# A gated attention and MLP decode step: the query weight loaded by eight transfers instead of one, the result written by four

## Chip, core and metric

The kernel runs on one core of a Trainium2 chip. A core has five engines that run their own instruction streams beside each other: TensorE (PE, matrix products; its weight loads are listed apart as PEld), VectorE (DVE), ScalarE (ACT), GpSimd (POOL) and SyncE (SP, which here only issues transfers). Sixteen DMA engines move data between the chip's main memory (HBM) and the on-chip buffer SBUF, which has 128 partitions. SP and ACT each have a queue from which they issue transfers. Engines wait for each other, and for transfers, by semaphores.

The metric is the device time of one execution in microseconds (us), the median of several. Lower is better.

## What is computed

One decode step for a batch of four tokens: attention over the last 4096 rows of a key and value cache, and a small gated MLP, mixed by a sigmoid gate. Cut to what matters:

```
B, D, Hq, Hkv, Dh, W, F = 4, 512, 32, 8, 128, 4096, 1792        # bfloat16
q      = (x @ wq)                       # wq: [512, 4096], 4 MB
scores = q . k_cache[:, :, -W:, :] * Dh ** -0.5
o      = softmax(scores) . v_cache[:, :, -W:, :]
a      = o @ wo                         # wo: [4096, 512], 4 MB
gate   = x @ W_gate;  up = x @ W_up
b      = (gate * (gate > 0) * up) @ W_down
g      = sigmoid((x * gate_w).sum(-1))
out    = g * a + (1 - g) * b            # [4, 1, 512]
```

The used parts of the two caches are 32 MB each, and the weights some 13 MB: about 81 MB are read in all, and 4 KB are written.

## The kernel before, in words

**Tiles and stages.** The eight sets `s` = 0 to 7 are half a batch entry each: four key/value heads of one token, 4 MB of keys and 4 MB of values. Keys lie in `Ksb` and values in `Vsb`, two buffers each, so that set `s + 2` can only be loaded when set `s` has been used. For each set, TensorE transposes the keys (`kt`, L340), ScalarE and VectorE copy the transposed tiles back into `Ksb` (L345, L347), TensorE makes the scores (L373), VectorE masks them (L381), ScalarE takes the exponentials (L410), VectorE transposes them (L417), and TensorE multiplies them with the values (L429) and combines the heads (L442). The MLP weights take the key and value buffers after the last sets.

**`Wbig`.** One tile of 128 partitions with 32 KB each holds `wq` at first. Row group `p` of `wq`, its rows 4p to 4p + 3, which are 32 KB in one piece, goes to partition `p`. When the query projection `qproj` (L457, 128 products) has read it, the same tile takes `wo`, in four transfers (`WO_CUTS`, L260).

**Order of the transfers.** All large ones are issued by SP, in the order of the program: `wq` (L245), K0, K1, V0, K2, V1 and so on (L236, L240), then the MLP weights (L250 to L255) and `wo`. ACT issues only two small ones at the start, the rows `x` (four rows of 1 KB, L243) and `gate_w` (one row, L244).

**How waits are written.** `P.op` and `P.dma` append to a list for each engine, with a name for the event and the names of events that it waits for. A DMA has a semaphore of its own (or one for its buffer), which counts 16 when it has landed. `plan` drops waits that an engine has already made. `P.op(engine, None, None, waits)` is a bare wait. Each engine's list becomes its instruction stream within one `nc.Block()`, at whose end the engines meet in a barrier that GpSimd gathers and releases.

**The start.** TensorE's first product (L306) waits for `x`, `gate_w` and an identity matrix that GpSimd makes; then come the gate (L315, L318, L319) and `qproj`, which waits for `("WQ",)`. The result of `qproj` goes through VectorE and TensorE (L461, L464, L468) and GpSimd (`place_q`, L357) to the scores of the first set, which also need K0.

**The end.** `gateup` and the last values are followed by the products with `W_down` (L545) and `wo` (L553), which add up in one bank of PSUM; VectorE copies it to `outs` (L557), a tile of 128 partitions of which every eighth holds a result row: row `8 b` of the 32 partitions of column block `c` has columns 128 c to 128 c + 127 of token `b`. SP writes these 16 pieces of 256 bytes with one transfer (L558) and waits for it (L559; the profile shows that wait under L562, the block's end). After that comes the barrier.

## Time and profile before

| what | value |
|---|---|
| median of 3 runs | 197.73 us (197.53 to 197.76) |
| the profiled execution, device time | 197.38 us |
| its span in the profile | 195.7 us |
| mean granted TensorE clock | 0.889 of full speed |
| busy: PE, DVE, ACT, POOL | 140.6, 103.6, 91.5, 7.9 us |
| read from HBM | 81.01 MB, 414 GB/s over the span |
| `wq` issued by SP, first product that reads it | 0.81 us, 13.08 us |
| last product, copy to `outs`, write issued by SP | 192.74, 193.19, 193.51 us |

The span runs from the first to the last instruction in the profile, and the device time has 197.38 - 195.7 = 1.7 us around it. Busy times of engines overlap, so they don't add up to the span. "PE busy" is the time in which matrix products were in the pipeline, whatever the clock.

### The profile page before, as it was taken

How to read it: one execution, taken by the hardware profiler on the slowest of the kernel's cores; microseconds unless marked ns; L12 is line 12 of the kernel's file. 1: busy time of each engine (PE TensorE's matmuls, PEld its weight loads, DVE VectorE, ACT ScalarE, POOL GpSimd, SP SyncE). 2: the span in 40 equal slices, each digit the busy share in tenths (PEclk: the TensorE clock that was granted, in tenths of full speed). 3: DMA queues.
4: the chain of work that ended last, by engine and by line, in shares of the span. 5: the costliest groups of instructions: out<-in, count | busy, mean ns of one | idle time of the engine just before them, and what ended most of it. 6: DMA issues, size and time to landing. Idle time of an engine off the chain costs nothing.

```text
span 195.7 us, 4263 instructions
## 1 busy us (share of the span) xinstructions
PE 140.6 (72%) x1858; PEld 107.7 (55%) x1858; DVE 103.6 (53%) x278; ACT 91.5 (47%) x108; POOL 7.9 (4%) x39
## 2 busy tenths in 40 slices
PE   0134199968889919992999399929992999498634
PEld 0034197535567518751976286528752875397533
DVE  2102025888599456945585659456945584741200
ACT  2000058698398409760886098509750976220000
POOL 7400000000000000000000000000000000000000
PEclk9999999999999996997599879996996699965855
DMA  6999999999999999999999999999999999999991
GB/s 215 449 429 452 429 449 442 425 429 437 432 422 429 425 429 429 427 429 425 435 429 435 429 429 430 429 429 429 429 429 429 435 411 425 450 431 415 422 385 59
DMA packets 3498, 81.19 MB, mean 415 GB/s; under 512 B 409, under 2 KB 414, under 8 KB 670
## 3 DMA queue, kind: packets, MB, share of 16 engines
q1 hardware_dynamic: 3476, 81.01, 96.8%
q8 instruction: 9, 0.15, 0.3%
q14 instruction: 3, 0.02, 0.0%
q10 hardware_dynamic: 10, 0.01, 0.0%
HBM read 81.01 MB, written 0.00 MB: 414 GB/s over the span
## 4 chain that ended last, share of the span: by engine, by line
DMA 57%; PE 25%; ACT 9%; DVE 4%; issue 1%; SPq 1%
DMA Ksb<-in_A_k_cache_dram 46%; PE bank L340 16%; DMA Wbig<-in_A_wo_dram 12%; ACT Ksb L345 7%; PE bank L373 5%; DVE Ksb L347 2%; PE bank L429 2%; ACT sc L410 2%; PE bank L553 1%; PE bank L442 1%; DVE pT L417 1%; ACT L410 1%; DVE sc L381 1%; SPq L260 0%; DVE oq L450 0%
## 5 line engine op out<-in xcount | busy, mean ns | idle before, releaser
L345 ACT ACTIVATE Ksb<-bank 128x1024 bf16<-128x1024 bf16 x72 | 70.9, 1022 | 68.2 <-PE bank L340 68.0
L340 PE MATMUL bank<-identf,Ksb 128*128 128x128 f32 x512 | 81.1, 313 | 29.4 <-DMA Ksb<-in_A_k_cache_dram 24.0
L340 PEld LDWEIGHTS bank<-identf,Ksb 128*128 128x128 f32 x512 | 66.6, 161 | 44.1 <-DMA Ksb<-in_A_k_cache_dram 25.7
L347 DVE COPY Ksb<-bank 128x1024 bf16<-128x1024 bf16 x56 | 38.0, 685 | 41.8 <-PE bank L340 40.8
L381 DVE CUSTOM_DVE_ANT_0 sc<-bank,mask 128x512 bf16<-128x512 f32 x32 | 21.7, 684 | 9.6 <-PE bank L373 9.5
L429 PE MATMUL bank<-Vsb,pT 128*32 128x256 bf16 x512 | 20.8, 291 | 0.9 <-DMA Vsb<-in_A_v_cache_dram 0.9
L373 PE MATMUL bank<-Ksb,QSP 128*32 128x512 bf16 x256 | 19.4, 383 | 2.1 <-DVE Ksb L347 1.6
L410 ACT ACTIVATE sc<-sc,negmax 128x1024 bf16<-128x1024 bf16 x16 | 18.3, 1146 | 4.8 <-DVE negmax L402 4.7
L417 DVE STREAM_TRANSPOSE pT<-sc 128x1024 bf16<-128x1024 bf16 x16 | 19.7, 1237 | 1.3 <-ACT sc L410 1.0
L429 PEld LDWEIGHTS bank<-Vsb,pT 128*32 128x32 bf16 x512 | 13.2, 101 | 7.1 <-issue 3.3
L442 PEld LDWEIGHTS bank<-osb,Wsel 128*64 128x64 f32 x128 | 8.1, 138 | 4.6 <-issue 2.6
L442 PE MATMUL bank<-osb,Wsel 128*64 128x32 f32 x128 | 8.9, 224 | 1.2 <-DVE osb L434 1.2
L373 PEld LDWEIGHTS bank<-Ksb,QSP 128*32 128x32 bf16 x256 | 4.1, 94 | 9.4 <-DVE Ksb L347 4.4
L477 PE MATMUL bank<-xT,Ksb 128*128 128x4 bf16 x112 | 6.9, 199 | 1.8 <-DVE oq L450 1.8
L477 PEld LDWEIGHTS bank<-xT,Ksb 128*128 128x128 bf16 x112 | 6.8, 160 | 1.9 <-issue 1.9
L553 PE MATMUL bank<-Wbig,oq 128*32 128x128 bf16 x128 | 4.2, 311 | 4.1 <-DMA Wbig<-in_A_wo_dram 4.0
L357 POOL COPY QSP<-QS 128x64 bf16<-128x64 bf16 x8 | 1.8, 236 | 118.2 <-PE bank L373 107.4
L457 PE MATMUL bank<-xT,Wbig 128*128 128x4 bf16 x128 | 3.6, 166 | 4.0 <-DMA Wbig<-in_A_wq_dram 4.0
L306 PE MATMUL bank<-ident,xsb 5*128 5x5 bf16 x4 | 0.3, 167 | 7.9 <-DMA xsb<-in_gate_w_dram 7.9
L553 PEld LDWEIGHTS bank<-Wbig,oq 128*32 128x32 bf16 x128 | 3.1, 140 | 5.0 <-DMA Wbig<-in_A_wo_dram 5.0
L457 PEld LDWEIGHTS bank<-xT,Wbig 128*128 128x128 bf16 x128 | 3.5, 104 | 4.0 <-DMA Wbig<-in_A_wq_dram 4.0
L434 DVE COPY osb<-bank 128x256 f32<-128x256 f32 x8 | 3.4, 420 | 3.6 <-PE bank L429 3.6
(55 smaller groups left out, 47.0 us busy)
## 6 DMA issues: line engine op xcount, KB each, us to landing
Ksb<-in_A_k_cache_dram SPq DMA_DIRECT2D x8, 4096.0 KB, 22.9
Vsb<-in_A_v_cache_dram SPq DMA_DIRECT2D x8, 4096.0 KB, 32.0
Wbig<-in_A_wq_dram SPq DMA_DIRECT2D x1, 4096.0 KB, 12.2
Wbig<-in_A_wo_dram SPq DMA_DIRECT2D x1, 2048.0 KB, 20.2
Ksb<-in_B_W_gate_dram SPq DMA_DIRECT2D x1, 1792.0 KB, 17.9
Ksb<-in_B_W_up_dram SPq DMA_DIRECT2D x1, 1792.0 KB, 21.8
Vsb<-in_B_W_down_dram SPq DMA_DIRECT2D x1, 1792.0 KB, 15.6
Wbig<-in_A_wo_dram SPq DMA_DIRECT2D x1, 1280.0 KB, 22.8
```

The source lines that it names most:

```text
L340: P.op("pe", lambda e, bk=bk, cc=cc, c=c, s=s: e.transpose(bk[:, cc * 128:(cc + 1) * 128], kw[:, c * 128:(c + 1) * 128], identf[:, :]), (" ...
L345: P.op("act", lambda e: e.activation(dst, bk[:, :].bitcast(BF16), ACTF.Copy), ("KTC", s, i), [("KT", s, i)])
L347: P.op("dve", lambda e: e.tensor_copy(dst, bk[:, :].bitcast(BF16)), ("KTC", s, i), [("KT", s, i)])
L373: P.op("pe", lambda e, a=a, h=h: e.matmul(bk[32 * a:32 * a + 32, 0:512], QSP[:, s % 2, h, :], k4[:, 16 * bank:16 * bank + 16, 32 * a:32 * ...
L381: P.op("dve", lambda e: e.tensor_tensor_reduce(sc[:, s % 2, bank * 512:(bank + 1) * 512], bk[:, :], mask[:, :], 1.0, LOWEST, ALU.add, ALU.max,
L410: P.op("act", lambda e: e.activation(sc[:, par, k * PW:(k + 1) * PW], sc[:, par, k * PW:(k + 1) * PW], ACTF.Exp, bias=negmax[:, par:par + ...
L417: P.op("dve", lambda e: e.transpose(pT[:, par, k * PW:(k + 1) * PW], sc[:, par, k * PW:(k + 1) * PW]), ("PTT", s, k), [("EXP", s, k), ("PV ...
L429: P.op("pe", lambda e, c=c, g=g, col=col: e.matmul(OB[32 * g:32 * g + 32, 0:256], pT[:, par, col:col + 32], v3[:, 16 * k + c, :], start=(k ...
L442: P.op("pe", lambda e, k=k, lo=lo: e.matmul(FB[r, 256:288], Wsel[:, lo:lo + 64], osb[:, par, 32 * k:32 * k + 32], start=(k == 0), stop=(k ...
L457: P.op("pe", lambda e, h=h, t=t: e.matmul(FB[:, 64 + 4 * h:68 + 4 * h], Wq3[:, t, 128 * h:128 * h + 128], xT[:, t * 8:t * 8 + 4], start=(t ...
L477: P.op("pe", lambda e, W=W, i=i, t=t, col=col: e.matmul(FB[:, col:col + 4], W[:, t, i:i + NFT * 127 + 1:NFT], xT[:, t * 8:t * 8 + 4], star ...
L553: P.op("pe", lambda e, i=i, cb=cb: e.matmul(AB[32 * cb:32 * cb + 32, 0:128], oq[:, i, :], Wo3[:, i, cb * 128:(cb + 1) * 128], start=False, ...
```

## The change

Three things are changed; the rest is the same.

```diff
-        P.dma("sp", lambda e: e.dma_start(Wbig[:, :], A_wq.rearrange("(p t) w -> p (t w)", p=128)), ("WQ",))
+        for r in range(8):
+            P.dma("sp", lambda e, r=r: e.dma_start(
+                Wbig[r:128:8, :], A_wq.rearrange("(e r t) w -> r e (t w)", r=8, t=4)[r]), ("WQ", r))
...
-                        ("Q",) if (h == HQ - 1 and t == 3) else None, [("WQ",), ("XTC",), ("G",)])
+                        ("Q",) if (h == HQ - 1 and t == 3) else None, [("WQ", r) for r in range(8)] + [("XTC",), ("G",)])
...
-        P.dma("sp", lambda e: e.dma_start(out.rearrange("b o (c d) -> c (b o) d", d=128), outs[0:128:8, :]), ("OUT",), [("OUTS",)])
-        P.op("sp", None, None, [("OUT",)])
+        for c in range(4):
+            P.dma(("sp", "act")[c % 2], lambda e, c=c: e.dma_start(
+                out[:, 0, 128 * c:128 * c + 128], outs[32 * c:32 * c + 32:8, :]), ("OUT", c), [("OUTS",)])
+        P.op("pool", None, None, [("OUT", c) for c in range(4)])
```

- `wq` is loaded by eight transfers of SP, one after the other. Transfer `r` moves 16 rows of 32 KB to the partitions r, r + 8, ..., r + 120. The eight have a semaphore each, and the first product of `qproj` waits for all of them. Each partition gets the same bytes as before.
- The result is written by four transfers of four rows of 256 bytes, one for each column block: SP issues blocks 0 and 2, ACT blocks 1 and 3. Both wait for the copy to `outs`.
- GpSimd, and no longer SP, waits for the result's transfers, with four semaphores, at the end of its list.

## The prediction

> **What bounds the kernel now.** I read the page's slices first, then its list of queues, its chain, the list of transfers, the windows at the start, and the timeline at both ends. The slices:

> ```profile
> PE   0134199968889919992999399929992999498634
> DMA  6999999999999999999999999999999999999991
> GB/s 215 449 429 452 429 449 442 425 429 437 432 422 429 425 429 429 427 429 425 435 429 435 429 429 430 429 429 429 429 429 429 435 411 425 450 431 415 422 385 59
> ...
> q1 hardware_dynamic: 3476, 81.01, 96.8%
> ```

> The DMA row is full from the second slice to the last but one, at about 430 GB/s whatever is moved, while every engine has gaps. SP's queue (q1) fills 96.8% of sixteen engines' time. So the kernel is one long stream of 81 MB, and it ends a fixed tail after the stream.

> ```profile
> DMA 57%; PE 25%; ACT 9%; DVE 4%; issue 1%; SPq 1%
> ...
> Ksb<-in_A_k_cache_dram SPq DMA_DIRECT2D x8, 4096.0 KB, 22.9
> Vsb<-in_A_v_cache_dram SPq DMA_DIRECT2D x8, 4096.0 KB, 32.0
> Wbig<-in_A_wq_dram SPq DMA_DIRECT2D x1, 4096.0 KB, 12.2
> ```

> The chain gives DMA only 57% because it follows compute wherever a buffer had to come free. The transfer list shows that this compute is not the limit: a key set takes 22.9 us to land and a value set 32.0, where 4 MB at 430 GB/s take 4.194 / 0.430 = 9.75 us. Each is issued while one or two others are still ahead of it, so the stream does not run dry. The shortest reserve is at SP's first wait, which ends at 36.99 us in the timeline: 16.8 MB had been issued by then and about (36.99 - 1.8) x 0.43 = 15.1 MB moved, so 1.7 MB or 3.8 us were left. A microsecond that the stream loses at its head is therefore a microsecond at the end: nothing later can catch up, since the stream is already full, and compute, which waits for it, moves along.

> The start and the end of the stream:

> ```profile
> 0.80 0.56 ACTq L243 DMA_DIRECT2D xsb<-in_A_x_dram  x1
> 0.81 0.39 SPq L245 DMA_DIRECT2D Wbig<-in_A_wq_dram  x1
> 1.26 1.34 SPq L236 DMA_DIRECT2D Ksb<-in_A_k_cache_dram  x2
> 1.40 0.23 ACTq L244 DMA_DIRECT2D xsb<-in_gate_w_dram  x1
> ...
> 193.19 0.29 DVE L557 CAST outs<-bank 128x128 bf16<-128x128 f32 x1 [8.29 <-PE bank L553]
> 193.51 0.69 SPq L558 DMA_DIRECT2D out_dram<-outs  x1
> ...
> SPq L562 <- DMA out_dram<-outs: 1.1, 1, 1.1
> ```

> ```profile
> 1.75:2.00 0.25, 0.00 (x0) 0.00 (x0) 0.25 (x3) 0.25 (x1) 0.25 (x2) 1.00 3.87 1065
> 2.00:2.25 0.25, 0.00 (x0) 0.00 (x0) 0.05 (x2) 0.25 (x1) 0.25 (x2) 1.00 3.23 918
> 2.25:2.50 0.25, 0.00 (x0) 0.00 (x0) 0.00 (x0) 0.25 (x1) 0.25 (x3) 1.00 0.40 131
> ```

> The windows book a packet where it began. A packet of `wq` is one row of 32 KB: 1065 GB/s in a quarter microsecond are 266 KB, so eight rows began in the first window, seven in the second, one in the third. Sixteen DMA engines took up their first row between 1.83 and 2.34 us (packet records): a stagger of 0.51 us.

> **The change part by part**, against the profiled 197.38 us (195.66 span and 1.72 around it), which is 0.35 us under the median of the runs shown.

> *1. Seven more issues on SP.* Rows: 0.39 us for `wq` now, 0.56 for the four rows of `x`, and 1.34 / 2 = 0.67 for a key set. Seven more cost 2.7 to 4.7 us, so K0, K1 and V0 are issued that much later: V0's issue, which ended at 3.24, ends at 6 to 8 us. The `wq` transfer covers this, since it keeps all sixteen engines in work until 12 us. An engine has a new row at least every 0.67 us and needs 1.2 us for one, so it does not run dry between the eight. Price 0; without this cover it would be up to 4.7 us.

> *2. Seven more semaphore packets per engine.* Packet records have them at 9 ns: 7 x 9 = +0.06 us.

> *3. The stagger of the first rows.* An engine may get its first row sooner when a transfer has one row per engine. Bounds: 0 and the whole 0.51 us. I take half, -0.25, as the second issue already follows within 0.4 to 0.7 us.

> *4. The pace of the rows.* Now a row takes 32.8 KB / (430 / 16 GB/s) = 1.22 us, eight rows per engine 9.75 us, and this pace is the same for keys, values and weights (429 to 435 GB/s in slice after slice). A pace that depends so little on what is moved is that of sixteen paths of fixed width. The profile doesn't tell whether they end at the DMA engines or at the partitions, because every large transfer in it goes to all 128 partitions. That is what the change gives up: source, row size and engines are as before, but at any time all sixteen engines now write to every eighth partition only. Lower bound: the paths are the engines' own, rows stay at 1.22 us, price 0. Upper bound: two engines meet on one path, and a row takes 2.44 us, as two streams through one resource do here: a key set with one set ahead of it (issued at 52.63, landed at 72.84) took 20.2 us, twice 9.75 and a little. Price 8 x 1.22 = +9.75 us. I take the upper end: the pace that the trace shows was measured with the full spread alone, and the spread is the one thing about the rows that is altered. The tiny `x` transfer, four rows of 1 KB into neighbouring partitions, speaks the other way (44 ns a row, like the single `gate_w` row), but 1 KB may fit in buffers on the way.

> [...]

> *5. What the first products wait for.* PE has eight semaphores to wait for in place of one; behind that wait stand all the rest of PE. A bare wait on PE is 51 ns in the trace, so at most 0.36 us. `qproj` and what follows end at 18.8 us, while the first transposes wait for K0 until 23.9: 5 us of cover. If `wq` lands late, K0 lands late after it, and the cover stays. Price 0; without the cover, +0.36.

> *6. The end.* Now: issue 0.69, wait 1.1, and 0.4 us to the end of the span. After: SP and ACT issue two each. The first costs about 0.56 (`x`, also four rows), the second between 0.23 (`gate_w`) and 0.56. With 0.05 between them the last issue ends 0.84 to 1.17 us after the start, +0.15 to +0.48 against 0.69. ACT has nothing else then; its last exponentials end at 172.4. GpSimd's wait replaces SP's: it has nothing behind it but its own part of the final barrier, which it gathers itself, so SP's signal (0.16 us from its wait's end to its drain) falls away, but a drain of its own (up to 0.32 in this trace) comes in. I take +0.3 - 0.1 = +0.2, bounds -0.0 and +0.65.

> Sum: 197.38 + 0.06 - 0.25 + 9.75 + 0.2 = 207.14, and with 0.35 for the median of the runs 207.5 us. With each bound at its end and the doubled rows kept, 197.73 + 0.06 + 9.75 + (-0.51 to 0) + (0 to 0.65) is 207.0 to 208.2. The first rows now take 1.6 to 2.1 us each, and part of this start-up (up to 0.9) may lie within the doubled time: 206.1. Own range 206.0 to 208.2.

> **The rivals.**

> *A. Rows keep their pace; gains and losses cancel.* For it: equal packet times, the `x` rows. Against: no transfer in the trace has this spread. Time: 197.73 + 0.06 - 0.25 + 0.2 = 197.7, within 0.2% of before (0.40 us, about what a measurement of this kernel can tell from no change). Chance 0.20.

> *B. Faster: the stagger goes and the end gets shorter.* One mechanism, at both ends of the stream: smaller transfers get under way sooner. All sixteen engines start at 1.83, -0.51; a write of four plain rows is issued in 0.23 rather than 0.56. Then the second issue ends at 0.23 + 0.05 + 0.23 = 0.51, -0.18, and GpSimd saves 0.16. Time: 197.73 + 0.06 - 0.51 - 0.18 - 0.16 = 196.9. It decides only if rows keep their pace and more than 0.4 us of these 0.85 come true. Against it: ACT's two issues at the start took 0.83 us together. Chance 0.14.

> *C. The change doesn't do what it says: two rows go to each of eight engines.* Transfers 0 to 3 would fill one half of the engines and 4 to 7 the other, which starts four issues later: 4 x 0.39 to 4 x 0.56 = 1.6 to 2.2 us. Nothing in the trace tells how 16 rows are dealt out. Time: 197.7 + 1.9 = 199.6. Chance 0.08.

> **How the numbers follow.** The forecast, doubled rows, has 0.58: the pace is that of fixed paths, and the partitions are what the change narrows. Predicted time 207.5. Leaving out half of B and the forecast's upper tail, 197.2 to 208.2 holds about 0.8. Slower: 0.58 + 0.08 + 0.06 from A's upper side = 0.72. Same: 0.14, the rest of A. Faster: B's 0.14.

> **What would show it.** Step 4: the first product of `qproj` starts at about 22.8 instead of 13.08, and the rate in the first ten microseconds after the start is near 215 GB/s, with packets of 2.4 us; K0's transposes then start near 33.6. If `qproj` starts near 13 us, step 4 is wrong, and A or B holds. If half of the rows come at full pace and the rest late, it is C. Step 3: the rows' first starts, in quarter microseconds. Step 1: no gap between the eight transfers. Step 6: from L557's end to the end of the span, 2.2 us now, about 2.4 after. The prediction is wrong as a whole if partitions don't matter to the pace, or if a late `wq` is caught up later, which the reserve of 3.8 us at SP's first wait would show growing.

## The result, and the profile after

The changed kernel takes 209.28 us (median of 6 runs, 208.98 to 209.42) against 197.53 us for the kernel before in the same session: 1.059 times as long (95% interval 1.058 to 1.061), 11.75 us more. The forecast was 207.5 with a range of 197.2 to 208.2. The direction and the main mechanism held, the size did not: the time lies 1.1 us above the range.

The slices of the changed kernel's page, 5.2 us each (PE busy, DMA busy, rate), and two lines of its list of queues and issues:

```profile
PE   0100333997898992999399949976993999596652
DMA  9999899999999999999999999999999999999980
GB/s 197 202 208 202 303 401 454 454 404 401 473 431 401 448 432 429 404 440 461 407 423 448 435 410 429 462 417 417 429 461 417 416 421 425 454 412 415 428 355 10
...
q1 hardware_dynamic: 3584, 81.01, 96.2%
...
Wbig<-in_A_wq_dram SPq DMA_DIRECT2D x8, 512.0 KB, 12.0
```

The DMA row is as full as before, but in the first four slices the rate is about 202 GB/s, where the second to the fourth slice of the kernel before had 429 to 452. This is a trap in reading such a page: "DMA 9" (the DMA engines busy for 90% of the slice or more) says that the engines had packets in hand, not that they moved them at their pace. Only the rate row shows the loss. From the sixth slice on, the stream runs as it did before.

The timeline of the changed kernel at the start and the end (start, duration, engine, line, what; in brackets the idle time before and what ended it):

```profile
0.81 5.03 SPq L246 DMA_DIRECT2D Wbig<-in_A_wq_dram  x8
5.88 1.25 SPq L236 DMA_DIRECT2D Ksb<-in_A_k_cache_dram  x2
24.05 3.56 PE L459 MATMUL bank<-xT,Wbig 128*128 128x4 bf16 x128 [16.15 <-DMA Wbig<-in_A_wq_dram]
...
204.02 0.29 DVE L559 CAST outs<-bank 128x128 bf16<-128x128 f32 x1 [8.29 <-PE bank L555]
204.34 1.49 SPq L561 DMA_DIRECT2D out_dram<-outs  x2
204.34 1.34 ACTq L561 DMA_DIRECT2D out_dram<-outs  x2
```

The first product that reads `wq` starts at 24.05 us instead of 13.08, 10.97 later, and the copy to `outs` at 204.02 instead of 193.19, 10.83 later: what was lost at the head of the stream is still missing 180 us later. From the start of that copy to the end of the span it was 195.66 - 193.19 = 2.5 us and is 207.7 - 204.0 = 3.7 us. Two losses, then: about 10.8 us at the head, 1.2 us at the end.

The packet records of the traces show the pace row by row (a packet of `wq` is one row of 32 KB; K0 is the first key set). Of 32 KB rows, each DMA engine's first of `wq` took 1.86 us on average before and 2.24 after; the second to fourth 1.21 and 2.56, the fifth 1.21 and 2.40, the sixth to eighth 1.21 and 2.55; K0's first row 1.21 and 1.75, its second 1.21 in both kernels.

### The profile page after: what moved, and what is told of

Same layout as the page of the kernel before. It is cut to its first block, busy times and chain, and to the rows that moved or that the text cites. A ratio compares the mean times of both kernels' runs of the same rounds, so it can differ in the third digit from the quotient of the medians.

```text
span 207.7 us, 4278 instructions
## 1 busy us (share of the span) xinstructions
PE 141.1 (68%) x1858; PEld 107.4 (52%) x1858; DVE 104.2 (50%) x278; ACT 91.7 (44%) x108; POOL 8.1 (4%) x39
## 3 DMA queue, kind: packets, MB, share of 16 engines
q1 hardware_dynamic: 3584, 81.01, 96.2%
HBM read 81.01 MB, written 0.00 MB: 390 GB/s over the span
## 4 chain that ended last, share of the span: by engine, by line
DMA 57%; PE 28%; ACT 8%; SPq 3%; DVE 1%; issue 1%
DMA Ksb<-in_A_k_cache_dram 46%; PE bank L342 17%; DMA Wbig<-in_A_wo_dram 11%; ACT Ksb L347 7%; PE bank L375 5%; SPq L246 2%; PE bank L431 2%; PE bank L444 2%; DVE Ksb L349 1%; ACT sc L412 1%; PE bank L555 1%; ACT L412 1%; SPq L262 0%; SPq L257 0%; DVE outs L559 0%
## 6 DMA issues: line engine op xcount, KB each, us to landing
Ksb<-in_A_k_cache_dram SPq DMA_DIRECT2D x8, 4096.0 KB, 23.2
Vsb<-in_A_v_cache_dram SPq DMA_DIRECT2D x8, 4096.0 KB, 31.9
```

## Experiments

All times are medians beside runs of the kernel before in the same session (197.5 to 197.7 us). Each kernel is the one before with the edit shown; where the load of `wq` is split, the first product waits for all its parts, as in the change.

### The two halves of the change, alone

`e1_wq_only` has the changed load of `wq` and the old write, `e2_out_only` the old load and the changed write.

```diff
# e1_wq_only
-        P.dma("sp", lambda e: e.dma_start(Wbig[:, :], A_wq.rearrange("(p t) w -> p (t w)", p=128)), ("WQ",))
+        for r in range(8):
+            P.dma("sp", lambda e, r=r: e.dma_start(
+                Wbig[r:128:8, :], A_wq.rearrange("(e r t) w -> r e (t w)", r=8, t=4)[r]), ("WQ", r))
# e2_out_only
-        P.dma("sp", lambda e: e.dma_start(out.rearrange("b o (c d) -> c (b o) d", d=128), outs[0:128:8, :]), ("OUT",), [("OUTS",)])
-        P.op("sp", None, None, [("OUT",)])
+        for c in range(4):
+            P.dma(("sp", "act")[c % 2], lambda e, c=c: e.dma_start(
+                out[:, 0, 128 * c:128 * c + 128], outs[32 * c:32 * c + 32:8, :]), ("OUT", c), [("OUTS",)])
+        P.op("pool", None, None, [("OUT", c) for c in range(4)])
```

> The kernel before with only the load of wq changed (eight transfers of 16 rows, every eighth partition). Theory 1 (pace: two DMA engines meet on one path into the partitions): rows of 2.55 us as in the changed kernel, the first product of the query projection at 24.0 us, the copy to outs 10.8 us later than before, time 208.2 to 208.6 us. Rival (the eight transfers cost little and most of the loss is the four writes and their wait): under 200 us.

> The kernel before with only the write of the result changed (four transfers, GpSimd waits). Theory: 1.0 to 1.3 us slower than before, 198.6 to 198.9 us: the last of four transfers begins 2.4 us after the first issue instead of 1.3, and GpSimd's waits and drain add 0.1 to 0.2. Rival, as predicted: +0.2 us, 197.8, if the late end in the changed kernel came from the late stream.

Measured: `e1_wq_only` 208.1 us, ratio 1.053 (1.051 to 1.055), +10.5 and 0.1 under the time expected; `e2_out_only` 198.91 us, ratio 1.007 (1.005 to 1.008), +1.3. The sum is 11.75, as much as the whole change costs. The halves don't touch each other, and the late end of the write is not a consequence of the late stream: it is there without it. The rival in the first expectation and "as predicted" in the second both fall. The write's issues in the timeline of `e2_out_only` take as long as in the whole change:

```profile
193.82 1.49 SPq L559 DMA_DIRECT2D out_dram<-outs  x2
193.82 1.34 ACTq L559 DMA_DIRECT2D out_dram<-outs  x2
```

### Is it the number of transfers, or what they reach?

`e3_wq_cols` keeps eight transfers and eight semaphores, but each goes to all 128 partitions, with an eighth of the columns.

```diff
-                Wbig[r:128:8, :], A_wq.rearrange("(e r t) w -> r e (t w)", r=8, t=4)[r]), ("WQ", r))
+                Wbig[:, 2048 * r:2048 * r + 2048], A_wq.rearrange("(p t) w -> p (t w)", p=128)[:, 2048 * r:2048 * r + 2048]), ("WQ", r))
```

> wq by eight transfers again, but each of all 128 partitions and an eighth of the columns (4 KB pieces). Theory 1 (partitions decide): packets of 4 KB at the pace of wo's, 159 ns, the whole of wq in about 10 us, time 197.5 to 198.3. Rival (the number of transfers and semaphores decides, whatever partitions they reach): 206 or more.

Measured: 198.09 us, ratio 1.004 (1.003 to 1.006), +0.5. From its page:

```profile
GB/s 205 421 444 428 424 434 441 431 441 429 431 441 441 418 441 428 413 428 438 428 441 428 428 428 428 429 434 428 428 434 428 428 410 428 452 423 417 428 381 53
```

The second slice nearly has the full rate, the third has it. Eight issues and 112 more semaphore packets cost next to nothing; the half microsecond is about the price of 4 KB pieces, eight of which take 8 x 159 ns = 1.27 us (159 ns is the median of `wo`'s 4 KB packets in the kernel before) where a 32 KB row takes 1.21 (8 x 0.06 = 0.5 us for each engine's share of `wq`).

### Is it the memory or the partitions?

`e4_src_block` leaves the partitions as in the change and reads neighbouring rows; `e5_dst_block` leaves the reads and writes neighbouring partitions.

```diff
# e4_src_block
-                Wbig[r:128:8, :], A_wq.rearrange("(e r t) w -> r e (t w)", r=8, t=4)[r]), ("WQ", r))
+                Wbig[r:128:8, :], A_wq.rearrange("(r e t) w -> r e (t w)", r=8, t=4)[r]), ("WQ", r))
# e5_dst_block
+                Wbig[16 * r:16 * r + 16, :], A_wq.rearrange("(e r t) w -> r e (t w)", r=8, t=4)[r]), ("WQ", r))
```

> Eight transfers to every eighth partition as in the change, but transfer r reads 16 neighbouring row groups of wq (512 KB in one piece) instead of every eighth: the rows of wq come to other partitions than x has, so the query is another one; amount and order of work are the same. Theory 1 (the partitions decide): rows of 2.55 us, 208.2 to 208.6 us, as with the change of wq alone. Rival (the memory decides: 16 reads 256 KB apart at a time meet in it): rows of 1.2 us, 197.5 to 198.3.

> The reads of the change (every eighth row group of wq) written to 16 neighbouring partitions, 16 r to 16 r + 15; the query is another one, amount and order of work are the same. [...] Rival (the step of 8 itself, or any transfer of 16 rows, has half the pace whichever the partitions): 208.

Measured: `e4_src_block` 207.83 us, ratio 1.052 (1.051 to 1.054), rows of 2.55 us (the time is 0.4 under the one expected); `e5_dst_block` 223.03 us, ratio 1.128 (1.126 to 1.130), rows of 4.52 us. The rates of `e4_src_block`, in slices of 5.2 us, and then of `e5_dst_block`, in slices of 5.6 us:

```profile
GB/s 205 204 204 204 305 417 477 426 407 410 464 441 404 420 455 426 426 418 433 442 433 414 439 433 445 409 439 433 433 426 414 458 401 415 457 445 392 430 393 68
```

```profile
GB/s 113 171 94 94 100 159 118 384 457 407 448 451 395 456 398 460 404 443 438 410 448 410 454 407 443 437 420 443 413 454 413 437 437 398 457 425 403 441 395 81
```

In `e5_dst_block` seven slices have 121 GB/s on average, then comes the full rate. Which rows are read makes no difference to the pace (2.55 us a row with either order); which partitions are written makes all of it. With 16 neighbours it is worse than with every eighth partition, 4.52 us a row against 2.55. The author's estimate for a quarter of the paths, 4 x 1.27 = 5.1 us a row (1.27 is half of the changed kernel's 2.55) and 226 to 230 us, was too high (the last section says what may lie behind it).

### Larger transfers, and other partitions

`e6_step4` uses 32 rows, every fourth partition; `e10_halves` two halves of 64 neighbours; `e11_step2in32` every second partition of a block of 32.

```diff
# e6_step4, four transfers
+                Wbig[r:128:4, :], A_wq.rearrange("(e r t) w -> r e (t w)", r=4, t=4)[r]), ("WQ", r))
# e10_halves, two transfers
+                Wbig[64 * r:64 * r + 64, :], A_wq.rearrange("(r e t) w -> r e (t w)", r=2, t=4)[r]), ("WQ", r))
# e11_step2in32, eight transfers
+                Wbig[32 * (r // 2) + r % 2:32 * (r // 2) + 32:2, :], A_wq.rearrange("(g e r t) w -> g r e (t w)", g=4, r=2, t=4)[r // 2, r % 2]), ("WQ", r))
```

> wq by four transfers of 32 rows, every fourth partition, two rows to an engine. All sixteen paths are reached by each transfer. Theory 1a (rows are dealt to engines in pairs of neighbours, r + 8 e and r + 8 e + 4, so that at any time the engines are again on every eighth partition): rows of 2.5 us at least at first, 206 to 209 us. Theory 1b (rows are dealt so that each engine keeps to one path): rows of 1.2 us, 197.5 to 198.5 us.

> wq by two transfers of 64 neighbouring partitions each, four rows to an engine in each. Theory (what counts is how many paths a transfer reaches: a half of the partitions reaches eight, whatever its number of rows and size): rows of 2.2 to 2.6 us, 205.5 to 208.5 us. Rival (only the small number of rows in a transfer slows it; 2 MB transfers run at full pace): 197.5 to 198.2 us.

> [...] Rival (two engines on a path give 25.7 GB/s, four give 29.0, wherever they write): rows of 2.55 us, 207.8 to 208.4 us.

Measured: `e6_step4` 197.89 us, ratio 1.002 (1.001 to 1.003); `e10_halves` 208.10 us, ratio 1.053 (1.052 to 1.055), rows of 2.56 us; `e11_step2in32` 208.17 us, ratio 1.054 (1.052 to 1.055), rows of 2.55 us. First the rates of `e6_step4`, then those of `e10_halves`:

```profile
GB/s 215 428 428 428 424 428 428 424 441 436 451 434 428 424 434 428 433 434 424 434 434 428 428 428 436 434 428 428 428 428 428 428 405 433 452 424 410 429 386 60
```

```profile
GB/s 192 216 203 203 305 403 419 470 426 410 419 465 410 426 422 451 426 424 419 442 432 432 419 438 438 434 413 438 438 438 413 438 409 422 459 438 398 421 396 72
```

Two transfers of 2 MB run at half of the rate (192 to 216 GB/s in the first four slices), four of 1 MB at the full rate (428). So neither the size of a transfer nor its number of rows decides. `e6_step4` also speaks for rows that are dealt out so that the sixteen engines don't meet (theory 1b): dealt as in theory 1a, they would at any time have been on every eighth partition, where the change has 202 GB/s. Its 0.4 us are about what the start lost: its first rows begin at 2.38 us on average, 0.36 later than before. `e11_step2in32` was to show whether 16 rows that lie closer together, within 32 partitions, move at another pace than 16 rows spread over all 128; they don't, at 2.55 us a row in both.

### The write

`e7_out_sp4` issues the four writes from SP alone, `e8_pool_wait` keeps one write and moves only the wait, `e12_two_writes` uses two writes of eight rows.

```diff
# e7_out_sp4
-            P.dma(("sp", "act")[c % 2], lambda e, c=c: e.dma_start(
+            P.dma("sp", lambda e, c=c: e.dma_start(
# e8_pool_wait
-        P.op("sp", None, None, [("OUT",)])
+        P.op("pool", None, None, [("OUT",)])
# e12_two_writes
+        for c in range(2):
+            P.dma(("sp", "act")[c], lambda e, c=c: e.dma_start(
+                out[:, 0, 256 * c:256 * c + 256].rearrange("b (c d) -> c b d", d=128), outs[64 * c:64 * c + 64:8, :]), ("OUT", c), [("OUTS",)])
+        P.op("pool", None, None, [("OUT", c) for c in range(2)])
```

> The four writes all issued by SP, GpSimd waits; wq as before. Theory (an issue takes 0.6 to 0.7 us of its queue and the queues work side by side): four in a row end 4 x 0.65 = 2.6 us after the start, the last packet 0.6 later, 1.0 to 1.3 us later than with two queues, 199.8 to 200.2 us. Rival (SP and ACT share what makes the packets, so two queues gain nothing): issues of 0.35 us, 198.7 to 199.1, as with two queues.

> One write by SP as before, but GpSimd waits for it instead of SP. Theory: GpSimd's wait and drain take about as long as SP's branch, drain and signal, -0.1 to +0.2 us, 197.5 to 197.8 us. Rival (the wait on GpSimd is what costs in the change): 198.3 or more.

> The result written by two transfers, one of SP and one of ACT, eight rows each; GpSimd waits for both; wq as before. Theory (an issue costs 0.6 to 0.75 us of its queue, the queues work side by side): both issues end about 0.75 us after the copy, 0.05 to 0.2 us later than one, and the second wait adds 0.05: 197.6 to 197.9 us, no gain. Rival (splitting the write shortens it, because each transfer has half of the rows): 197.2 or less.

Measured: `e7_out_sp4` 199.54 us, ratio 1.011 (1.009 to 1.012), +2.0 and 0.3 under the time expected; `e8_pool_wait` 197.60 us, ratio 1.000 (0.999 to 1.001); `e12_two_writes` 197.84 us, ratio 1.001 (1.000 to 1.002). The issues in the timelines of `e7_out_sp4` and then of `e12_two_writes`:

```profile
193.23 0.29 DVE L557 CAST outs<-bank 128x128 bf16<-128x128 f32 x1 [7.44 <-PE bank L553]
193.55 2.68 SPq L559 DMA_DIRECT2D out_dram<-outs  x4
```

```profile
193.67 0.67 SPq L559 DMA_DIRECT2D out_dram<-outs  x1
193.68 0.64 ACTq L559 DMA_DIRECT2D out_dram<-outs  x1
```

Four issues on one queue end 2.68 us after their start, two and two on both queues 1.49: the queues work side by side, if not without any loss (0.58 to 0.75 us an issue on one queue, 0.60 to 0.75 on two). Each issue costs its queue about 0.65 us, whether it moves four rows, eight or sixteen (0.69 in the kernel before), so every additional round of issues is paid in full here, where nothing is left to hide it. Moving one wait to GpSimd costs nothing that can be measured. No version of the load or of the write was faster than the kernel before.

## Why the prediction missed, step by step

| step | predicted, us | measured, us | from |
|---|---|---|---|
| 2, semaphore packets | +0.06 | about +0.1, within the rows | 15 to 24 ns each instead of 9 |
| 3, first rows begin | -0.25 | +0.45 | 2.02 on average before, 2.47 after |
| 4, eight rows of `wq` | +9.75 | +9.63 | 10.35 before, 19.98 after |
| 4, K0's first row | 0 | +0.54 | 1.21 before, 1.75 after |
| 6, the write | +0.2 | +1.2 to +1.3 | spans; `e2_out_only` |
| sum | +9.76 | +11.8 to +11.9 | 11.75 by the medians, 12.0 by the spans |

Of the 2.1 us by which the predicted sum falls short, 1.0 to 1.1 are step 6, 0.7 step 3 and 0.5 K0's first row; step 4, by far the largest term, was right to 0.1 us.

**What held.** The kernel is bound by the stream, and a loss at its head is one at the end: +10.97 us at the first product of the query projection, +10.83 at the copy to `outs`. Step 1 held too: eight issues took 0.63 us each, K0 was issued 4.6 us later, and no gap appeared in the packets. So did step 5: the products that wait for `wq` still end before K0 lands (29.8 and 34.7 us in the timeline).

**Step 4, the pace.** No run had shown the doubled row when it was forecast: the 9.75 us were the author's estimate, and the runs show 9.63. The upper end was the right one, and the side on which the pace is set is now shown: it is that of the partitions (`e4_src_block`, 2.55 us a row as in the change; `e5_dst_block`, 4.52), as by paths that the rows share. Its size came out nearly right by two errors that cancel. A shared row takes 2.55 us, not 2 x 1.22, which makes eight rows longer; the start-up of the first row, 0.65 us of its 1.86, hides in the doubled time, which makes them shorter. What was left out, put at nothing without a word, is K0's first row, +0.54 us: it took 2.12 us on the engine that came to it first and 1.36 on the one that came last. That fits engines that leave the shared paths one after the other, so that those ahead still share with those behind; no run tried it apart.

The ways of loading `wq` tried here fall into three groups. The full rate, 428 GB/s or so, goes with all 128 partitions at a time (the kernel before, `e3_wq_cols`) and with every fourth (`e6_step4`). About half of it, 202 to 204 GB/s on average over the first four slices and rows of 2.55 or 2.56 us, goes with every eighth partition (the change, `e4_src_block`) and with 64 neighbours (`e10_halves`); 16 partitions out of 32 neighbours have the same row of 2.55 us (`e11_step2in32`). About a quarter, 121 GB/s and rows of 4.52 us, goes with 16 neighbours (`e5_dst_block`). If these are sixteen, eight and four paths, which is an estimate from the rates, then 16 x 32,768 B in 2.55 us are 206 GB/s over eight paths, 25.7 each, and in 4.52 us 116 GB/s over four, 29.0 each. The second figure may flatter the paths, as the last section says. Which partitions share a path was not shown one by one.

**Step 3, the first rows: wrong in sign.** It assumed that the stagger comes from dealing out eight rows per engine, so that a transfer with one row each would start faster. The windows of the changed kernel at the start (the last column is the rate, booked where a packet began):

```profile
1.75:2.00 0.25, 0.00 (x0) 0.00 (x0) 0.25 (x3) 0.25 (x1) 0.25 (x2) 1.00 0.05 16
2.00:2.25 0.25, 0.00 (x0) 0.00 (x0) 0.05 (x2) 0.25 (x1) 0.25 (x2) 1.00 2.76 655
2.25:2.50 0.25, 0.00 (x0) 0.00 (x0) 0.00 (x0) 0.25 (x1) 0.25 (x3) 1.00 3.49 786
2.50:2.75 0.25, 0.00 (x0) 0.00 (x0) 0.00 (x0) 0.25 (x1) 0.25 (x2) 1.00 0.54 131
2.75:3.00 0.25, 0.00 (x0) 0.00 (x0) 0.00 (x0) 0.23 (x1) 0.25 (x2) 1.00 2.17 524
```

No row begins before 2.0 us, where eight did before; then come five, six, one and four. The stagger grew (2.20 to 2.99 us instead of 1.83 to 2.34), and the first transfer's issue took 0.62 us instead of 0.39. The two go together: in the runs whose first issue took 0.58 to 0.65 us the first rows begin at 2.38 to 2.54 us on average, in the kernel before, in the runs that keep its load of `wq` and in `e5_dst_block`, where it took 0.39 or 0.40, at 1.97 to 2.15. What makes an issue longer is open, and with it the cause of this term: 0.39 to 0.49 for the 128-row pieces of `e3_wq_cols` (one of the eight took 0.62) and for the 16 neighbouring partitions of `e5_dst_block`; 0.56 to 0.66 for 16 rows with a step of 8 or 2, 32 with a step of 4, and 64 neighbours.

**Step 6, the write: the largest miss, a term mis-sized by 1.0 to 1.1 us.** The second issue was priced between 0.23 (one row, `gate_w`) and 0.56 (`x`); it took 0.70 on SP, and the first 0.75. That makes 1.49 us instead of 0.84 to 1.17, +0.80 against the single write. Two more parts were put at nothing or at a gain: the wait from the end of the last issue to the landing is 1.30 us instead of 1.07, +0.23, and GpSimd ends its four waits 0.15 us after the first of them, +0.15. Together 1.2. A row that could have warned was in the same profile: the single write's own issue, 0.69 us for 4 KB, was longer than that of every load of 4 MB but one (0.80 us, L240). The prediction priced the new issues by the loads of `x` and `gate_w` instead.

**The range.** Its upper end took the bounds of steps 3 and 6 as they stood. For step 3 that was a gain of 0 at the least, so a later start was ruled out without a reason. With the 0.45 us that the start in fact lost, and a second write issue at 0.69 (+0.74 with the 0.05 between), the upper end would have been 197.73 + 0.06 + 9.75 + 0.45 + 0.74 + 0.17 for GpSimd = 208.9, and 209.4 with K0's row.

## What to carry to other kernels

## What was not expected of the hardware

At half pace the sixteen engines move a little less than half: by the estimate of two engines on each of eight paths, a pair moves 25.7 GB/s in all (rows of 2.55 us), one engine alone 27.0 (rows of 1.21). Rows within 32 partitions (`e11_step2in32`, 2.55 us) or within 64 (`e10_halves`, 2.56) lose as much as rows spread over all 128 (the change, 2.55); why pairs lose was not tried further. The engines stayed in step in the changed kernel: sixteen rows that start within 0.8 us end within 1.2 us of each other after eight rows.

By the same estimate four engines on one path would move more, 29.0 GB/s in `e5_dst_block`, but that is not shown. Each of its rows goes to another block of 16 partitions than the row before, and the engines begin a row up to 1.4 us apart, so some may already write to other paths while the rest still share the old ones. A smaller gain, which may be of this kind, shows in `e10_halves`: its fifth row, the first in the other 64 partitions, took 2.39 us, the rows on both sides of it 2.56. In the changed kernel the fifth row took 2.40, and it is as short in all the runs at half pace (2.36 to 2.40). If every row of `e5_dst_block` gains by such a change of paths, 4.52 us is less than four engines need that stay on one path. A load that keeps four engines on the same path for several rows would settle it; none was run.
